# First feed-forward layer of chunk pairs by seven block products, with weight blocks kept in DRAM

## The chip, the cores and the metric

One core of a Trainium2 chip runs the whole kernel. The metric is the device time of one execution in microseconds (us); the time quoted for a kernel is the median of several executions. The engines are named as in the profile: PE is TensorE's matmul, PEld its weight load, DVE VectorE, ACT ScalarE, POOL GpSimd, SP SyncE, which here only issues DMAs.

## What is computed

```python
# attention: batch 4, heads 8, sequence 768, head dim 64, blocks of 64
for b in range(nb):                       # decayed linear attention
    intra = (qb @ kb.T * Dmask) @ vb
    inter = (qb * lam_pow) @ kv_state
    out[b] = intra + inter
    kv_state = lam_block * kv_state + (kb * rev_pow).T @ vb
# feed-forward on the 3072 tokens: d_model 512, d_ff 2048
x = attn_out.transpose(0, 2, 1, 3).reshape(3072, 512)
h = x @ w_in                              # 512 -> 2048, the first layer
g = softplus(h)
return g @ w_out                          # 2048 -> 512, the second layer
```

All is float32 in and out. Each of the large products is taken as three products of rounded parts: an operand is split in a high part (fp32r) and a low part (the rest, fp32r), and high·high, low·high and high·low are summed.

## The kernel before

The sequence is cut in `NCH` = 6 chunks of 128 positions; a chunk has 4 batches × 128 = 512 tokens. The hidden width is cut in `NF` = 16 blocks f of 128. A **step** s stands for chunk s // 16 and block s % 16, so there are 96 steps. The order is written by hand: every engine runs its instructions in the order in which the program emits them, and waits where a tile isn't there yet.

In step s the program emits, in this order: the decays of the attention unit that comes next, if one comes in step s + 1 (`k_decay` on ACT, `q_decay` on DVE); the softplus chain of step s − 1 (`chain_act` and `chain_hi` on ACT, `chain_lo` on DVE); up to step 16 the conversion of the weights (below); the second layer of step s − 4 (`mlp2`, 12 matmuls); an attention unit, if one is due; the first layer of step s (`mlp1`, 12 matmuls); and the DMA issues on SP's queue (`w_load`, `load_upto`).

**Attention** has 24 units g, one for each chunk and pair of heads (4 to a chunk). `mm_scores` and `mm_out` are runs of 64×64 matmuls. `mask_scores` and `update_states` follow `mm_scores` on DVE, and `mm_out` of a unit reads what both of them wrote. From unit 9 on, a unit is an event in `both_at`: in one step `mm_out` of unit g − 1 and `mm_scores` of unit g, every fourth step (g = 9 in step 19, g = 23 in step 75); `x_high` and `x_low` then write the high and low parts of the chunk's x. Unit 8 has its scores in step 17. `load_upto(n)` issues the loads of the units below n, two DMAs of 512 KB each; the load of unit 9 is emitted at the end of step 17.

**Weights** arrive as 64-bit words. Group j (two of the 32 weight blocks) is converted in step j and finished in step j + 1: `w_scale` and `w_round` on ACT, then `w_shift`, `w_sign`, `w_add` on DVE, and a step later `w_hi` on ACT and `w_lo` on DVE. In step s the emitted order is `w_hi` of group s − 1, `w_scale` and `w_round` of group s, `w_lo` of group s − 1, `w_shift`, `w_sign`, `w_add` of group s, and only then the attention unit's `mask_scores` and `update_states`. The last group, 15, is finished in step 16. The converted weights (16 tiles) stay in SBUF to the end.

**Buffers.** Tiles of 8 KB per partition come from one pool of 21 slots (`t8`): raw and converted weight pairs, x (two tiles to a chunk), attention units, output tiles. A tile's first writer waits until the last user of the slot's former tile is done. Tiles of 4 KB come from a pool of 7 (`t4`): the g of a step, conversion scratch. PSUM has four banks for the second layer's sums, two of kind `bank` (h, and an event's x and y), and one two-bank tile `work` (`mm_out`'s z, and the scores of the units outside events).

Of the kernel before, what the change touches and what calls it, by code (L numbers as in the profile page):

```python
# [31 lines left out]
def decay_attention_softplus_ffn(  # L32
# [264 lines left out]
    def mm_scores(g, x, y):  # L297
        q, k, kd, v = q_of(g), k_of(g), kds.pop(g), vt_of(g)
        if first_chunk(g):

            nc.tensor.matmul(y[lo], lhsT=warm[hi, :64], rhs=warm[hi], start=True, stop=False)
        for b in range(B):
            for t in range(2):
                cols = slice((2 * b + t) * 64, (2 * b + t + 1) * 64)
                for s in range(2):
                    r = half(s)
                    nc.tensor.matmul(x[r, cols], lhsT=k[r, b, t], rhs=q[r, b, t], start=True, stop=True)  # L307
                    if s == 0 or not last_chunk(g):
                        nc.tensor.matmul(  # L309
                            y[half(1 - s), cols], lhsT=kd[r, b, t], rhs=v[r, b, t],  # L310
                            start=s == 0 or not first_chunk(g), stop=s == 0 or not first_chunk(g),
                        )


    def mm_out(g, w):
        a, qd, v, st = aa.pop(g), qds.pop(g), vt_of(g), states[g]
        for b in range(B):
            cols = slice(b * 64, b * 64 + 64)
            for s in range(1 if first_chunk(g) else 0, 2):
                r = half(s)  # L320
                for t in range(2):
                    nc.tensor.matmul(w[half(t), s, cols], lhsT=st[r, b, t], rhs=qd[r, b, t], start=True, stop=False)  # L322
            for s in range(2):
                r = half(s)
                for t in range(2):
                    nc.tensor.matmul(  # L326
                        w[half(t), s, cols], lhsT=v[r, b, t], rhs=a[r, b, t],
                        start=s == 0 and first_chunk(g), stop=True,
                    )
# [45 lines left out]

    def x_low(g, w):
        x = x_of(g // NP, g % NP).rearrange("q n (b s i) -> q n s b i", b=B, s=2)
        nc.vector.tensor_sub(  # L378
            out=x[:, 1], in0=w[:, :, 0:256].rearrange("q s (b i) -> q s b i", b=B), in1=x[:, 0]
        )  # L380
# [4 lines left out]
    def chain_act(s):  # L385
        l_tiles[s] = tl([128, 512], F32, f"l{s}")
        nc.scalar.activation(l_tiles[s], h_tiles.pop(s), AF.Softplus)  # L387

    def chain_hi(s):
        g_tiles[s] = t4([128, 2, 512], F32R, f"g{s}")  # L390
        nc.scalar.copy(out=g_tiles[s][:, 0, :], in_=l_tiles[s])  # L391

    def chain_lo(s):
        g = g_tiles[s]
        nc.vector.tensor_sub(out=g[:, 1, :], in0=l_tiles.pop(s), in1=g[:, 0, :])  # L395

    def mlp1(s, ps_=range(NP)):
        c, f = divmod(s, NF)
        if s not in h_tiles:
            h_tiles[s] = bank(f"h{s}")  # L400
        w = w_of(f, 0)
        for p in ps_:
            cs = slice(p * 128, (p + 1) * 128)
            x = x_of(c, p)
            for n, (i, j) in enumerate(((0, 0), (1, 0), (0, 1))):
                nc.tensor.matmul(  # L406
                    h_tiles[s], lhsT=w[:, i, cs], rhs=x[:, j, :],
                    start=p == 0 and n == 0, stop=p == NP - 1 and n == 2,
                )

    def mlp2(ss):
        c = ss[0] // NF
        ends = ss[-1] % NF == NF - 1
        if ss[0] % NF == 0:
            o_tiles[c] = [obank(f"o{c}_{b}") for b in range(B)]
        if ends:
            ob = t8([128, B, 512], F32, f"ob{c}")
        for b in range(B):
            for s in ss:
                f = s % NF  # L420
                g, w = g_tiles[s], w_of(f, 1)
                for n, (i, j) in enumerate(((0, 0), (0, 1), (1, 0))):
                    nc.tensor.matmul(  # L423
                        o_tiles[c][b], lhsT=g[:, i, b * 128 : (b + 1) * 128], rhs=w[:, j],
                        start=f == 0 and n == 0, stop=f == NF - 1 and n == 2,
                    )
# [16 lines left out]
    xy, z = {}, {}  # L443
# [31 lines left out]

    last = NCH * NF
# [4 lines left out]
    outs_at[4 * NG - 17] = NG - 1  # L483
    units_at = {**scores_at, **both_at}
    for s in range(LAG, last + LAG):
        if s + 1 in units_at:
            k_decay(units_at[s + 1])
            q_decay(units_at[s + 1])
        if s - 1 < last:
            chain_act(s - 1)  # L490
            chain_hi(s - 1)
            chain_lo(s - 1)
# [12 lines left out]
        if s == last + LAG - 2:  # L505
            mlp2([s - LAG, s - LAG + 1])
        elif s - LAG < last - 1 and s - 1 not in both_at:
            mlp2([s - LAG])
        if s in scores_at:
            scores_of(scores_at[s])  # L510
            if scores_at[s] == 2 * NP:
                keep_values(2 * NP)
        if s in both_at:

            g = both_at[s]
            w, x, y = work(f"z{g - 1}"), bank(f"x{g}"), bank(f"y{g}")
            mm_out(g - 1, w)
            mm_scores(g, x, y)
            mask_scores(g, x)
            x_high(g - 1, w)  # L520
            update_states(g, y)
            x_low(g - 1, w)
            if g < NG - 1:
                keep_values(g)
# [52 lines left out]
```

## Time and profile before

| | us |
|---|---|
| median of 3 executions | 607.62 (607.26 to 607.64) |
| the profiled execution, first to last instruction | 606.2 |
| PE busy | 596.9 |
| DVE busy | 226.4 |
| ACT busy | 219.8 |
| POOL busy | 4.7 |

The profiled execution's span is 606.2 us; what lies around the instructions, some 1.4 us, is the difference to the median. A row of a group shows line, engine, operation, output<-input by the program's names, shape and count, then busy time in us and the mean of one in ns, then the engine's idle time ahead of these instructions and what ended it. A row of the timeline shows start in us, duration in us, engine, line, operation, and in brackets the idle time before it and what ended that. A busy PE is not PE at its peak, since matmuls overlap; so their pace is read from the distance between starts.

### The profile page before, as it was taken

Reading aid. Unit: us, or ns where it says so; the run is one execution under the profiler, and the core shown is the slowest. Engines: PE = TensorE matmul, PEld = TensorE weight load, DVE = VectorE, ACT = ScalarE, POOL = GpSimd, SP = SyncE. Lnnn points to the kernel's source line nnn. Section 1 sums busy time; section 2 is a strip of 40 time slices with the busy share of each in tenths; the row PEclk is TensorE's granted clock in tenths of the full one; section 3 lists DMA queues with packets and bytes.
Section 4 is the critical chain, followed back from the end, with each engine's and each line's share of the span. In section 5 each row is a group of like instructions: output and inputs, shape, how many; then the busy total and the mean of one; then the engine's idle time right before and its main releaser. Section 6 shows DMA issues by size and latency. Waiting matters only on the chain.

```text
span 606.2 us, 11776 instructions
## 1 busy us (share of the span) xinstructions
PE 596.9 (98%) x5299; PEld 488.5 (81%) x5299; DVE 226.4 (37%) x336; ACT 219.8 (36%) x355; POOL 4.7 (1%) x11
## 2 busy tenths in 40 slices
PE   9899999999999999999999999999999999999997
PEld 6577888888888888888888888888888888888886
DVE  7779999853232233132222321321312211211111
ACT  3777777633222223332223323222333121322121
POOL 3000000000000000000000000000000000000000
PEclk9999999999999999999999999999999999999999
DMA  8995314216002023300120500211500000100001
GB/s 297 406 406 227 122 74 141 88 52 208 3 2 70 1 70 98 112 2 11 61 70 29 182 2 0 71 32 40 207 3 1 1 1 1 69 2 0 1 0 69
DMA packets 15169, 48.98 MB, mean 81 GB/s; under 512 B 1808, under 2 KB 1808, under 8 KB 15120
## 3 DMA queue, kind: packets, MB, share of 16 engines
q1 hardware_dynamic: 14832, 47.72, 21.8%
q8 instruction: 41, 0.67, 0.4%
q10 hardware_dynamic: 288, 0.52, 0.2%
q14 instruction: 8, 0.07, 0.0%
HBM read 41.95 MB, written 6.29 MB: 80 GB/s over the span
## 4 chain that ended last, share of the span: by engine, by line
PE 91%; DMA 7%; DVE 1%; SPq 1%; ACT 0%; issue 0%
PE o L423 43%; PE h L406 41%; DMA raw<-in_wts 5%; PE z L322 2%; PE x L307 2%; DMA att<-in_att 2%; PE z L326 2%; PE w L307 1%; PE y L309 1%; SPq L84 0%; DVE w L238 0%; DVE c L231 0%; DVE c L225 0%; SPq L126 0%; ACT w L234 0%; PE w L309 0%
## 5 line engine op out<-in xcount | busy, mean ns | idle before, releaser
L423 PE MATMUL o<-w,g 128*128 128x512 f32 x1152 | 278.9, 391 | 1.1 <-DVE w L238 0.8
L406 PE MATMUL h<-x,w 128*128 128x512 f32 x1152 | 276.8, 391 | 0.0
L423 PEld LDWEIGHTS o<-w,g 128*128 128x128 f32 x1152 | 215.0, 188 | 47.2 <-DVE w L238 1.1
L406 PEld LDWEIGHTS h<-x,w 128*128 128x128 f32 x1152 | 215.1, 188 | 46.7 <-issue 1.2
L395 DVE TENSOR_TENSOR g<-l,g 128x512 fp32r<-128x512 f32 x96 | 66.4, 692 | 310.4 <-ACT g L391 310.2
L387 ACT ACTIVATE l<-h 128x512 f32<-128x512 f32 x96 | 57.4, 598 | 309.0 <-PE h L406 306.4
L391 ACT CAST g<-l 128x512 fp32r<-128x512 f32 x96 | 59.6, 621 | 3.1
L371 ACT CAST x<-z 128x512 fp32r<-128x512 f32 x24 | 14.0, 585 | 41.4 <-PE z L326 41.4
L334 DVE TENSOR_TENSOR a<-x,mask 128x512 f32<-128x512 f32 x15 | 10.4, 692 | 36.1 <-PE y L309 26.4
L339 DVE SCALAR_TENSOR_TENSOR st<-st,lam_c,y 64x256 f32<-64x256 f32 x52 | 22.9, 480 | 0.8
L322 PEld LDWEIGHTS z<-qd,st 64*64 64x64 f32 x640 | 17.0, 134 | 7.0 <-issue 7.0
L307 PE MATMUL x<-att 64*64 64x64 f32 x608 | 21.9, 219 | 0.0
L213 ACT ACTIVATE c<-raw 128x1024 f32<-128x1024 f32 (+1 forms) x19 | 19.0, 1001 | 7.3 <-DMA raw<-in_wts 7.3
L234 ACT CAST w<-c 128x1024 fp32r<-128x1024 f32 (+1 forms) x19 | 17.4, 914 | 10.3 <-DVE c L231 7.7
L238 DVE TENSOR_TENSOR w<-c,w 128x1024 fp32r<-128x1024 f32 (+1 forms) x19 | 20.0, 1053 | 2.8 <-ACT w L234 2.7
L231 DVE CUSTOM_DVE_ANT_0 c<-raw,c 128x2048 uint16<-128x2048 uint16 (+1 forms) x19 | 20.1, 1058 | 2.4
L322 PE MATMUL z<-qd,st 64*64 64x64 f32 x640 | 20.9, 224 | 0.0
L307 PEld LDWEIGHTS x<-att 64*64 64x64 f32 x608 | 20.0, 135 | 1.0 <-PE z L326 0.5
L225 DVE SCALAR_TENSOR_TENSOR c<-raw,c 128x1024 uint32<-128x1024 uint32 (+1 forms) x19 | 20.1, 1056 | 0.6
L378 DVE TENSOR_TENSOR x<-z,x 128x512 fp32r<-128x512 f32 x24 | 16.6, 690 | 7.9 <-ACT x L371 7.5
L217 ACT ACTIVATE raw<-raw 128x1024 uint32<-128x1024 uint32 (+1 forms) x19 | 18.9, 993 | 0.0
L285 ACT ACTIVATE kd<-att,rp 128x256 f32<-128x256 f32 x40 | 18.1, 502 | 0.0
(54 smaller groups left out, 230.5 us busy)
## 6 DMA issues: line engine op xcount, KB each, us to landing
att<-in_att SPq DMA_DIRECT2D x48, 512.0 KB, 5.5
raw<-in_wts SPq DMA_DIRECT2D x32, 512.0 KB, 10.2
out_dram<-ob SPq DMA_DIRECT2D x22, 256.0 KB, 2.2
out_dram<-ob ACTq DMA_DIRECT2D x2, 256.0 KB, 2.0
lam_b<-in_lam SPq DMA_DIRECT2D x1, 4.0 KB, 2.6
```

Source lines behind the costliest of these rows:

```text
L213: nc.scalar.activation(c.bitcast(F32), raw_at(ks, 1).bitcast(F32), AF.Copy, scale=2.0**-112)
L225: nc.vector.scalar_tensor_tensor(out=c, in0=raw_at(ks, 1), scalar=0x80000000, in1=c, op0=ALU.bitwise_and, op1=ALU.bitwise_or)
L231: nc.vector.tensor_add(out=c, in0=c, in1=raw_at(ks, 0))
L238: nc.vector.tensor_sub(out=w[:, 1], in0=conv.pop(ks[0]).bitcast(F32), in1=w[:, 0])
L307: nc.tensor.matmul(x[r, cols], lhsT=k[r, b, t], rhs=q[r, b, t], start=True, stop=True)
L322: nc.tensor.matmul(w[half(t), s, cols], lhsT=st[r, b, t], rhs=qd[r, b, t], start=True, stop=False)
L339: nc.vector.scalar_tensor_tensor(out=to[:, :, t], in0=of[:, :, t], scalar=lam_c[r, h : h + 1], in1=u[:, :, t], op0=ALU.mult, op1=ALU.add,)
L387: nc.scalar.activation(l_tiles[s], h_tiles.pop(s), AF.Softplus)
L391: nc.scalar.copy(out=g_tiles[s][:, 0, :], in_=l_tiles[s])
L395: nc.vector.tensor_sub(out=g[:, 1, :], in0=l_tiles.pop(s), in1=g[:, 0, :])
L406: nc.tensor.matmul(h_tiles[s], lhsT=w[:, i, cs], rhs=x[:, j, :], start=p == 0 and n == 0, stop=p == NP - 1 and n == 2,)
L423: nc.tensor.matmul(o_tiles[c][b], lhsT=g[:, i, b * 128 : (b + 1) * 128], rhs=w[:, j], start=f == 0 and n == 0, stop=f == NF - 1 and n == 2,)
```

## The change

The step loop ends after two chunks (`STD` = 2), 32 steps. Chunks 2+3 and 4+5 go in pairs: for 8 pairs of hidden blocks, the 2×2 block product (two hidden blocks by two chunks, the contraction of 512 cut in two halves) is formed by seven products of sums of blocks, `P1` to `P7`, in place of eight. A product is 6 matmuls (2 slices of the contraction × 3 parts). Their sums of outputs run on PSUM and DVE. The second layer of the first chunk of a pair is emitted among the products of the next iteration (`rest`); that of the second chunk follows in a loop of its own, whose softplus outputs wait in SBUF.

The blocks of w_in and their sums S1 to S4, split in parts, and w_out, go to DRAM tiles `g1`, `g2`, `g3` during steps 8 to 31 (`store_blocks`, `block_sums` on POOL, `store_sums`), and are loaded again in each iteration (`load_w1`, `load_w2`). In SBUF only the iteration's blocks are held.

The attention events come twice as often: unit 8's scores in step 15 in place of 17, units 9 to 16 every second step from 16 to 30, and units 17 to 23 one to an iteration of the first pair. The load of unit 9 is emitted at the end of step 14. For chunks 2 to 5 `x_raw` copies x unsplit, and `x_sums_early`, `x_sums_late` and `x_block` form and split the sums of x (T1 to T4) on DVE and ACT.

```diff
+STD = 2
+    dr = ctx.enter_context(tc.tile_pool(name="dr", bufs=1, space=bass.MemoryType.DRAM))
...
+    g1 = [dr.tile([128, 2, 4, 256], F32, name=f"g1_{i}", tag=f"g1_{i}") for i in range(NF // 2)]
+    g2 = [dr.tile([128, 2, 3, 256], F32, name=f"g2_{i}", tag=f"g2_{i}") for i in range(NF // 2)]
+    g3 = [dr.tile([128, 2, 2, DM], F32, name=f"g3_{i}", tag=f"g3_{i}") for i in range(NF // 2)]
...
+    def block_sums(i):
+        full = t4([128, 2, DM], F32, f"full{i}")
+        for n in range(2):
+            w = w_of(2 * i + n, 0)
+            nc.gpsimd.tensor_add(out=full[:, n], in0=w[:, 0], in1=w[:, 1])
...
+        sums = block_parts[i] = t4([128, 4, 256], F32, f"sums{i}")
+        nc.gpsimd.tensor_add(out=s1, in0=a21, in1=a22)
+        nc.gpsimd.tensor_sub(out=s3, in0=a11, in1=a21)
+        nc.gpsimd.tensor_sub(out=s2, in0=s1, in1=a11)
+        nc.gpsimd.tensor_sub(out=s4, in0=a12, in1=s2)
+    def store_sums(i):
+        sums = block_parts.pop(i)
+        parts = t8([128, 2, 4, 256], F32R, f"parts{i}")
+        nc.scalar.copy(out=parts[:, 0], in_=sums)
+        nc.vector.tensor_sub(out=parts[:, 1], in0=sums, in1=parts[:, 0])
...
+    def load_w1(i):
+        a, b = t8([128, 2, 4, 256], F32R, f"w1a{i}"), t8([128, 2, 3, 256], F32R, f"w1b{i}")
+        nc.sync.dma_start(out=a.bitcast(F32), in_=g1[i])
+        nc.sync.dma_start(out=b.bitcast(F32), in_=g2[i])
...
+    def product(name, i, to, start=True):
+        a, n = W_AT[name]
+        w, x = w1_tiles[i][a], xc[name]
+        for p in range(2):
+            for m, (k, j) in enumerate(((0, 0), (1, 0), (0, 1))):
+                nc.tensor.matmul(
+                    to, lhsT=w[:, k, n, p * 128 : (p + 1) * 128], rhs=x[:, j, p],
+                    start=start and p == 0 and m == 0, stop=p == 1 and m == 2, skip_group_check=True,
+                )
...
-    scores_at[NF + 1] = 2 * NP
-    both_at = {4 * g - 17: g for g in range(2 * NP + 1, NG)}
+    scores_at[NF - 1] = 2 * NP
+    both_at = {2 * g - 2: g for g in range(2 * NP + 1, 4 * NP + 1)}
...
         if s in units_at:
             load_upto(units_at[s] + 2)
+        if s == NF - 2:
+            load_upto(2 * NP + 2)
+        if 8 <= s < 8 + NF:
+            store_blocks(s - 8)
+        if s >= NF and s % 2 == 0:
+            block_sums((s - NF) // 2)
+        if s >= NF and s % 2:
+            store_sums((s - NF) // 2)
...
+        for i in range(NF // 2):
+            if i + 1 < NF // 2:
+                load_w1(i + 1)
+            load_w2(i)
+            unit = nxt if more else None
+            if unit is not None and unit < NG:
+                k_decay(unit)
+                q_decay(unit)
...
+            product("P1", i, a)
+            nc.scalar.copy(out=p1, in_=a)
+            product("P6", i, b_)
+            nc.vector.tensor_add(out=u2, in0=b_, in1=p1)
+            product("P5", i, c_)
+            product("P2", i, a, False)
+            la = tl([128, 512], F32, f"la{c}_{i}")
+            nc.scalar.activation(la, a, AF.Softplus)
+            ga = parts_of(f"g{c}_{2 * i}", la)
+            product("P7", i, b_, False)
+            nc.vector.tensor_add(out=u3, in0=b_, in1=p1)
+            nc.vector.tensor_add(out=u3, in0=c_, in1=u3)
+            nc.scalar.activation(lb[2 * i + 1], u3, AF.Softplus)
+            low_of(ga, la)
+            run(rest, 2)
+            product("P4", i, b_, False)
+            nc.vector.tensor_add(out=c21, in0=b_, in1=p1)
+            nc.scalar.activation(c21, c21, AF.Softplus)
+            gb = parts_of(f"g{c}_{2 * i + 1}", c21)
+            product("P3", i, c_, False)
+            nc.vector.tensor_add(out=u2, in0=c_, in1=u2)
+            nc.scalar.activation(lb[2 * i], u2, AF.Softplus)
+            run(rest, 4)
+            if unit is not None and unit <= NG:
+                event(unit)
+                load_upto(unit + 2)
+                nxt += 1
+            low_of(gb, c21)
+            run(rest)
+            pair = [(2 * i + n, (ga, gb)[n], w2_tiles[i][:, n]) for n in range(2)]
+            rest = seconds(c, pair, i == NF // 2 - 1)
```

More of the change, by code (lines that the diff above doesn't have):

```diff
@@ L374, in x_high, with x_raw @@
         )
+    xr = {}
+    def x_raw(g, w):
+        c, p = divmod(g, NP)
+        if c not in xr:
+            xr[c] = t8([128, NP, 512], F32, f"xr{c}")
+        nc.scalar.copy(
+            out=xr[c][:, p].rearrange("q (b s i) -> q s b i", b=B, s=2),
+            in_=w[:, :, 0:256].rearrange("q s (b i) -> q s b i", b=B),
+        )
     def x_low(g, w):
@@ new lines, in decay_attention_softplus_ffn, with x_sums_early, x_sums_late @@
+    t_sums = {}
+    def x_sums_early(c, n):
+        out = t_sums[n] = t8([128, 4, 512], F32, f"tt{c}_{n}")
+        nc.vector.tensor_sub(out=out[:, 0], in0=xr[c + 1][:, n], in1=xr[c][:, n])
+        x_block("P5", out[:, 0], n)
+    def x_sums_late(c, n):
+        tt = t_sums.pop(n)
+        b12, b22, b21 = xr[c + 1][:, n], xr[c + 1][:, 2 + n], xr[c][:, 2 + n]
+        nc.vector.tensor_sub(out=tt[:, 1], in0=b22, in1=tt[:, 0])
+        nc.vector.tensor_sub(out=tt[:, 2], in0=b22, in1=b12)
+        nc.vector.tensor_sub(out=tt[:, 3], in0=b21, in1=tt[:, 1])
+        x_block("P6", tt[:, 1], n)
+        x_block("P7", tt[:, 2], n)
+        x_block("P4", tt[:, 3], n)
+        x_block("P3", b22, n)
@@ new lines, in product, with parts_of @@
+    def product(name, i, to, start=True):
[6 more added lines that the diff above has]
+                    start=start and p == 0 and m == 0, stop=p == 1 and m == 2, skip_group_check=True,
+                )
+    def parts_of(name, l):
+        g = t4([128, 2, 512], F32R, name)
+        nc.scalar.copy(out=g[:, 0], in_=l)
+        return g
@@ new lines, in low_of, with second, finish @@
+    def low_of(g, l):
+        nc.vector.tensor_sub(out=g[:, 1], in0=l, in1=g[:, 0])
+    outs, obs = {}, {}
+    def second(c, f, b, g, w):
+        if (c, b) not in outs:
+            outs[c, b] = obank(f"o{c}_{b}")
+        for n, (i, j) in enumerate(((0, 0), (0, 1), (1, 0))):
+            nc.tensor.matmul(
+                outs[c, b], lhsT=g[:, i, b * 128 : (b + 1) * 128], rhs=w[:, j],
+                start=f == 0 and n == 0, stop=f == NF - 1 and n == 2,
+            )
+    def finish(c, b):
+        if c not in obs:
+            obs[c] = t8([128, B, 512], F32, f"ob{c}")
+        copy = nc.vector.tensor_copy if b % 2 else nc.scalar.copy
+        copy(out=obs[c][:, b], in_=outs[c, b])
+        queue = nc.scalar if c == NCH - 1 and b % 2 == 0 else nc.sync
+        queue.dma_start(out=out[b * S + c * C : b * S + (c + 1) * C, :], in_=obs[c][:, b])
@@ new lines, in seconds, with run @@
+    def seconds(c, fs, ends=False):
+        work_ = []
+        for f, g, w in fs if not ends else ():
+            work_ += [lambda f=f, g=g, w=w, b=b: second(c, f, b, g, w) for b in range(B)]
+        if ends:
+            for b in range(B):
+                for f, g, w in fs:
+                    work_.append(lambda f=f, g=g, w=w, b=b: second(c, f, b, g, w))
+                work_.append(lambda b=b: finish(c, b))
+        return work_
+    def run(work_, n=None):
+        for _ in range(len(work_) if n is None else min(n, len(work_))):
+            work_.pop(0)()
@@ L479, in decay_attention_softplus_ffn, with event @@
+    last = STD * NF
     scores_at = {3 * n + 3: NP + n for n in range(NP)}
     outs_at = {s + 2: g for s, g in scores_at.items()}
-    scores_at[NF + 1] = 2 * NP
-    both_at = {4 * g - 17: g for g in range(2 * NP + 1, NG)}
-    outs_at[4 * NG - 17] = NG - 1
+    scores_at[NF - 1] = 2 * NP
+    both_at = {2 * g - 2: g for g in range(2 * NP + 1, 4 * NP + 1)}
     units_at = {**scores_at, **both_at}
-    for s in range(LAG, last + LAG):
+    def event(g):
+        w = work(f"z{g - 1}")
+        mm_out(g - 1, w)
+        if g < NG:
+            x, y = bank(f"x{g}"), bank(f"y{g}")
+            mm_scores(g, x, y)
+            mask_scores(g, x)
+        x_raw(g - 1, w)
+        if g < NG:
+            update_states(g, y)
+            keep_values(g)
@@ L486, in decay_attention_softplus_ffn @@
+    for s in range(LAG, last):
         if s + 1 in units_at:
@@ L488, in decay_attention_softplus_ffn @@
             q_decay(units_at[s + 1])
[L489 to L492, printed above, removed]
+        chain_act(s - 1)
+        chain_hi(s - 1)
+        chain_lo(s - 1)
         old, new = w_group(s - 1), w_group(s)
@@ L504, in decay_attention_softplus_ffn @@
             w_add(*new)
-        if s == last + LAG - 2:
-            mlp2([s - LAG, s - LAG + 1])
-        elif s - LAG < last - 1 and s - 1 not in both_at:
+        if s - 1 not in both_at:
             mlp2([s - LAG])
@@ L513, in decay_attention_softplus_ffn @@
         if s in both_at:
[L515 to L524, printed above, removed]
+            event(both_at[s])
             mlp2([s + 1 - LAG])
@@ L536, in decay_attention_softplus_ffn @@
             load_upto(units_at[s] + 2)
+        if s == NF - 2:
[6 more added lines that the diff above has]
+            store_sums((s - NF) // 2)
+        for at, name, n in ((23, "P1", 0), (23, "P1", 1), (25, "P2", 0), (25, "P2", 1)):
+            if s == at:
+                x_block(name, xr[2][:, n + (2 if name == "P2" else 0)], n)
+        if s == last - 3:
+            x_sums_early(2, 0)
@@ new lines, in decay_attention_softplus_ffn, with old_seconds @@
+        if s == last - 2:
+            x_sums_late(2, 0)
+            load_w1(0)
+        if s == last - 1:
+            x_sums_early(2, 1)
+    x_sums_late(2, 1)
+    chain_act(last - 1)
+    chain_hi(last - 1)
+    chain_lo(last - 1)
+    def old_seconds(ss, ends=False):
+        return seconds(STD - 1, [(s % NF, g_tiles[s], w_of(s % NF, 1)) for s in ss], ends)
+    for b in range(B):
+        outs[STD - 1, b] = o_tiles[STD - 1][b]
+    run(old_seconds([last - 4, last - 3]))
+    rest = old_seconds([last - 2, last - 1], True)
@@ new lines, in decay_attention_softplus_ffn, with split @@
+    nxt = 4 * NP + 1
+    for c in range(STD, NCH, 2):
+        more = c + 2 < NCH
+        lb = {}
+        gs = {}
+        for i in range(NF // 2):
[6 more added lines that the diff above has]
+                q_decay(unit)
+            if i % 2 == 0:
+                l4 = t8([128, 4, 512], F32, f"lb{c}_{i}")
+            for n in range(2):
+                lb[2 * i + n] = l4[:, 2 * (i % 2) + n]
+            ta, tb = t4([128, 2, 512], F32, f"ta{c}_{i}"), t4([128, 2, 512], F32, f"tb{c}_{i}")
+            p1, u2, u3, c21 = ta[:, 0], ta[:, 1], tb[:, 0], tb[:, 1]
+            a, bc = bank(f"a{c}_{i}"), work(f"bc{c}_{i}")
+            b_, c_ = bc[:, 0], bc[:, 1]
+            product("P1", i, a)
[29 more added lines that the diff above has]
+            rest = seconds(c, pair, i == NF // 2 - 1)
+        ahead = 2
+        def split(f):
+            gs[f] = parts_of(f"g{c + 1}_{f}", lb[f])
+            low_of(gs[f], lb[f])
+        for f in range(ahead):
+            split(f)
+        for i in range(2):
+            load_w2(i)
+        run(rest)
+        xc.clear()
+        steps = []
+        if more:
+            steps = [lambda n=n, m=m: x_block(n, xr[c + 2][:, m + (2 if n == "P2" else 0)], m) for n in ("P1", "P2") for m in range(2)]
+            for n in range(2):
+                steps += [lambda n=n: x_sums_early(c + 2, n), lambda n=n: x_sums_late(c + 2, n)]
+        for f in range(NF - 2):
+            if f % 2 == 0 and f // 2 + 2 < NF // 2:
+                load_w2(f // 2 + 2)
+            if f + ahead < NF:
+                split(f + ahead)
+            if f >= 1:
+                run(steps, 1)
+            if f == 9 and more:
+                load_w1(0)
+            run(seconds(c + 1, [(f, gs.pop(f), w2_tiles[f // 2][:, f % 2])]))
+        rest = seconds(c + 1, [(f, gs[f], w2_tiles[f // 2][:, f % 2]) for f in (NF - 2, NF - 1)], True)
@@ L539, in _layout @@
+    run(rest)
 def _layout(q, k, v, lam, w_in, w_out):
```

31 lines of the change are left out of this document (28 added, 3 removed).

## The prediction

> **What bounds the kernel now.** I read the page's busy line first, then the chain that ended last, then the costliest groups, and at last the timeline of single engines where the change moves work.
>
> ```profile
> PE 596.9 (98%) x5299; PEld 488.5 (81%) x5299; DVE 226.4 (37%) x336; ACT 219.8 (36%) x355; POOL 4.7 (1%) x11
> PE 91%; DMA 7%; DVE 1%; SPq 1%; ACT 0%; issue 0%
> L423 PE MATMUL o<-w,g 128*128 128x512 f32 x1152 | 278.9, 391 | 1.1 <-DVE w L238 0.8
> L406 PE MATMUL h<-x,w 128*128 128x512 f32 x1152 | 276.8, 391 | 0.0
> ```
>
> PE is busy for 98% of the span and makes 91% of the chain; its two large groups idle 1.1 us in all. So a matmul that goes shortens the span by its pace, as long as nothing new makes PE wait. The pace isn't the 391 ns of the rows, as matmuls overlap. It is read from the chain in order of time, whose columns are start, length and what ran:
>
> ```profile
> 144.71 5.44 PE h L406 x24
> ...
> 168.82 5.44 PE h L406 x24
> ...
> 591.58 10.89 PE o L423 x48
> ```
>
> 48 matmuls take 10.89 us and 24 take 5.44: **0.2267 us each**, for both layers, although the second layer changes its PSUM bank every three matmuls. From one event to the next, four steps on, it is 168.82 - 144.71 = 24.11 us; four steps of 24 matmuls are 21.76, so an event costs PE 2.35 us. The change keeps the number of events, so their cost stays.
>
> **What is removed.** The first layer of chunks 2 to 5 has 4 x 16 x 12 = 768 matmuls now. After it is 2 pairs x 8 iterations x 7 products x 6 = 672. So 96 matmuls go: 96 x 0.2267 = **21.8 us**. The second layer keeps its 1152. Whether PE gives all of this to the span depends on what it may have to wait for, place by place.
>
> **Inside an iteration** (the handing over of PSUM). The sums on DVE and ACT cost what the rows of the same size show:
>
> ```profile
> L395 DVE TENSOR_TENSOR g<-l,g 128x512 fp32r<-128x512 f32 x96 | 66.4, 692 | 310.4 <-ACT g L391 310.2
> L387 ACT ACTIVATE l<-h 128x512 f32<-128x512 f32 x96 | 57.4, 598 | 309.0 <-PE h L406 306.4
> L391 ACT CAST g<-l 128x512 fp32r<-128x512 f32 x96 | 59.6, 621 | 3.1
> L339 DVE SCALAR_TENSOR_TENSOR st<-st,lam_c,y 64x256 f32<-64x256 f32 x52 | 22.9, 480 | 0.8
> L285 ACT ACTIVATE kd<-att,rp 128x256 f32<-128x256 f32 x40 | 18.1, 502 | 0.0
> ```
>
> An iteration is 42 + 24 = 66 matmuls, 14.96 us, and with an event 17.3. DVE has seven operations of 0.69 in it (u2 twice, u3 twice, c21, two low parts), 4.8 us, and with an event 3.3 more (mask 0.69, four updates of 0.48, q_decay 0.69): 8.1 of 17.3. ACT has 4 evictions or softplus at 0.6 and so on, seven operations, 4.3 us, and 2.2 with an event. Neither is a bound. The tightest handing over is P4, which accumulates on P7's bank and must wait until DVE has read it into u3: six second-layer matmuls lie between, 1.36 us, against one DVE operation of 0.69 and two wake-ups. A wake-up from PE to ACT is near 0.04 us in the trace (the h group that starts at 121.87 and lasts 2.88 ends at 124.75, ACT starts at 124.79; both rows stand further down). I take nothing; the bound is 0.5 us in each of 16 iterations, 8 us, if a wake-up were half a microsecond.
>
> **The reloads.** Per iteration SP loads 1.05 + 0.79 MB of w_in blocks and sums and 1.05 MB of w_out, in the first pair also a unit of 1.05 MB: 3.93 MB in 17.3 us, 227 GB/s; in the second pair 2.88 MB in 14.96 us, 193 GB/s; in the loops of the second chunk 1.05 MB per 5.44 us, 193 GB/s.
>
> ```profile
> GB/s 297 406 406 227 122 74 141 88 52 208 3 2 70 1 70 98 112 2 11 61 70 29 182 2 0 71 32 40 207 3 1 1 1 1 69 2 0 1 0 69
> DMA to landing us min/median/max: 3.4/4.9/7.8
> ```
>
> The first row is the page's, 40 slices; the second is of the issues of attention loads from 140 to 480 us. The second and third slices held 406 GB/s of loads, so the need is about half of what the queue has shown, and each load is issued an iteration ahead. Stores (22 MB over steps 8 to 31, some 149 us, 148 GB/s) have less need. Cost: nothing.
>
> **The entry to the first pair.** After the last x of unit 15, DVE and ACT form 7 sums and parts for each half of T1 to T4. Counting from the end of the scores in step 30, DVE has mask and updates (2.6), `x_sums_late` (4.8), the step's low part, the split of the last block sums (1.2), `x_sums_early` (1.4) and two operations more of the second `x_sums_late` ahead of P6's: some 14 us. PE has 12 + 12 + 12 + 24 + 6 + 3 matmuls ahead of the one that needs it, 15.6 us. It fits by about 1.5 us, so I take nothing, with a bound of 4 us, the whole of an `x_sums_late` late.
>
> **Steps 14 to 16.** Here the change moves work onto work, and here I expect a wait. Unit 8's scores and the event of unit 9 come in steps 15 and 16 (17 and 19 before), while weight groups 14 and 15 are still being converted. Rows of ACT, DVE, PE and SP's queue from the timeline of the kernel before, and one of the waits of SP's queue:
>
> ```profile
> 110.99 1.05 ACT L234 CAST w<-c 128x1024 fp32r<-128x1024 f32 x1 [2.59 <-PE z L326]
> 116.56 1.06 ACT L234 CAST w<-c 128x1024 fp32r<-128x1024 f32 x1 [0.81 <-DVE c L231]
> 119.59 0.91 ACT L285 ACTIVATE kd<-att,rp 128x256 f32<-128x256 f32 x2
> 124.79 0.60 ACT L387 ACTIVATE l<-h 128x512 f32<-128x512 f32 x1 [1.60 <-PE h L406]
> 115.30 1.23 DVE L231 CUSTOM_DVE_ANT_0 c<-raw,c 128x2048 uint16<-128x2048 uint16 x1
> 116.44 0.68 DVE L378 TENSOR_TENSOR x<-z,x 128x512 fp32r<-128x512 f32 x1
> 117.65 1.23 DVE L238 TENSOR_TENSOR w<-c,w 128x1024 fp32r<-128x1024 f32 x1
> 118.79 0.69 DVE L221 TENSOR_SCALAR c<-c 128x1024 uint32<-128x1024 uint32 x1
> 119.52 1.22 DVE L225 SCALAR_TENSOR_TENSOR c<-raw,c 128x1024 uint32<-128x1024 uint32 x1
> 120.88 1.23 DVE L231 CUSTOM_DVE_ANT_0 c<-raw,c 128x2048 uint16<-128x2048 uint16 x1
> 129.34 1.79 DVE L339 SCALAR_TENSOR_TENSOR st<-st,lam_c,w 64x256 f32<-64x256 f32 x4
> 113.71 2.88 PE L423 MATMUL o<-w,g 128*128 128x512 f32 x12
> 116.43 2.88 PE L406 MATMUL h<-x,w 128*128 128x512 f32 x12
> 121.87 2.88 PE L406 MATMUL h<-x,w 128*128 128x512 f32 x12
> 124.59 2.88 PE L423 MATMUL o<-w,g 128*128 128x512 f32 x12
> 128.50 3.02 PE L406 MATMUL h<-x,w 128*128 128x512 f32 x12
> 119.35 0.80 SPq L84 DMA_DIRECT2D att<-in_att  x2
> SPq L84 <- PE h L406: 9.3, 1, 9.3
> ```
>
> The 21 slots of 8 KB are all taken in step 14: weight pairs 0 to 13, four x tiles, unit 8, the raw words of groups 14 and 15. The rows confirm it: `w_hi` of group 13 waited 2.59 us for `mm_out` of unit 7 (110.99), and the load of unit 9 waited 9.3 us, to 119.35, for the end of step 15's first layer (116.43 + 2.88), which frees chunk 0's x. After the change that load is emitted in step 14. It is the first to ask for the slot of raw group 14, free when `w_add` 14 ends, 115.30 + 1.23 = 116.5. In the kernel before, `w_hi` 14 started at that very moment (116.56), on that slot; now it must wait for chunk 0's x.
>
> Now the chain, in the times of this trace. Issue of the load 116.55, of its second half about 116.95, landing 4.9 later: 121.85. In ACT's order `k_decay` 9 stands ahead of the softplus chain of step 14, and that ahead of `w_hi` 14: 0.91 + 0.62 + 0.62, so `w_hi` 14 starts near 124.0 (its slot is free by 121.2). From `w_hi` 14 to the end of `w_add` 15 it is 120.88 + 1.23 - 116.56 = 5.55 us, at the same spacing. Queued behind that on DVE are `mask_scores` 8 (0.69) and the first two updates of the state (2 x 0.45), which `mm_out` 8 reads: 124.0 + 7.15 = **131.2**.
>
> PE meanwhile: second layer of step 11 at 113.71, to 116.43; the scores of unit 8 need the `work` tile, which `x_low` 7 frees at 117.12 (0.7 late); they take 128.50 - (124.59 + 2.72) = 1.2; first layer of step 15 with 2.85, to 121.2; second layer of step 12, to 123.9. Then `mm_out` 8 must wait until 131.2: **7.3 us**, and 0.7 before. With landings of 3.4 and 7.8 us in place of 4.9 the stall is 5.8 or 10.2. Afterwards DVE and ACT catch up: an event comes every 13.2 us, in which DVE has some 7 us. The loads of units 10 to 12 come a step ahead of their use behind the stores of `parts`; I find them 4 to 8 us ahead of what PE needs.
>
> POOL's sums are 2 + 4 operations every two steps:
>
> ```profile
> 6.80 1.84 POOL L292 TENSOR_TENSOR own<-att,lp 64x512 f32<-64x512 f32 x1 [4.40 <-DVE lam_c L183]
> 10.59 1.28 POOL L292 TENSOR_TENSOR own<-att,lp 64x512 f32<-64x512 f32 x1 [1.95 <-DMA att<-in_att]
> ```
>
> At 1.56 us for 512 columns and half for 256 that is 6.2 us of 13.2; it stays hidden.
>
> The Trainium skill, "SBUF — State Buffer", section "Who interferes with whom", says that a DVE instruction with two SBUF inputs and a GpSimd instruction that reads SBUF exclude each other, the later one blocking fully. The first four-part sum of POOL would fall on the stretch of `w_lo`, `w_sign`, `w_add`; by the rule, three waits of up to 0.8 us (half of 1.56) would make the stall up to 2.4 us longer, 596.3. The trace of before has POOL at work in its first 12 us alone and doesn't decide it.
>
> **The sum.** 607.6 - 21.8 + 0.7 + 7.3 = **593.8, say 594 us**. The profiled execution spans 606.2, its median stands 1.4 higher, and the new span would be 592.4.
>
> **Rivals.**
>
> 1. *No stall in step 16*, if unit 9's load finds another slot or group 15's conversion is ordered earlier than I count: 607.6 - 21.8 = 586 to 588. Against it stands the full table of slots. Chance 0.16.
>
> 2. *The stall slows PE behind it.* The longest wait of PE in the list of waits is 1.4 us (the row gives the sum, the count and the longest), so no long one is shown; but its first matmuls have a slow start:
>
> ```profile
> PE z L326 <- issue: 2.4, 2, 1.4
> 1.45 7.12 PE L146 MATMUL warm_ps<-warm 128*128 128x512 f32 x18 [1.45 <-DVE warm L141]
> ```
>
> 18 matmuls took 7.12 us where the later pace gives 4.08. If 7 us of waiting bring that back, up to 3.0 us are added: 595 to 597. Chance 0.26. This is the rule of the Trainium skill, "TensorE: Matmul & The Clock Gate", section "What's actually happening": after an idle window of about 3.4 us the clock halves, and a window of work restores it; by its figures, as an estimate, 1.7 us.
>
> 3. *The handing over of PSUM isn't covered*: 0.3 to 0.8 us in each of 16 iterations, 5 to 13 us beside the stall: 599 to 607. For it speaks the short cover of P4, against it the small wake-up. Chance 0.08.
>
> 4. *Slower than before: the reloads come late.* All of it hangs on the rate of loads while stores and output run beside them. The gain that is left, 13.7 us, is used up where the rate falls to about 207 GB/s (3.93 MB then takes 19.0 in place of 17.3 us, eight times). At 180 GB/s an iteration of the first pair takes 21.8 and one of the second 16.0 us: +36 and +8, 638 us. The 406 GB/s speak against it; that no store of this size is in the trace leaves it open. Chance 0.06.
>
> The forecast has 0.42; 0.02 is left for something else. The range leaves out rival 4 and the upper half of rival 3, and reaches to rival 1: **586 to 601**, about 0.86 by these cases, which I leave so, since the stall's size is unsure on both sides. Faster by over 0.2% (what can be told from no change) has 0.91, within it 0.02, slower 0.07.
>
> **What would show it.** Right: 96 fewer matmuls of the first layer; steps and products at 0.2267 us; one PE idle of 6 to 10 us near 124 us, ahead of z, ended by DVE, with `k_decay` 9 waiting for the load of unit 9; the granted clock after it tells rival 2. Wrong: PE waiting ahead of P4 or P7 on DVE (rival 3), or weight loads of the products waiting on DMA (rival 4), or POOL ending most waits of ACT's copy in `store_sums`.

## The result and the profile after

| | us | ratio to before, 95% interval |
|---|---|---|
| before | 607.63 (607.26 to 607.76) | |
| changed | **651.35** (649.75 to 651.98) | 1.0716 [1.07, 1.0731] |

Each row is the median of four executions, with the lowest and the highest.

The change makes the kernel 7% slower; 594 was forecast, with 586 to 601 as the range. The profiled execution took 651.41 us, its span is 649.6.

From the page of the changed kernel, the busy line and the chain by engine:

```profile
PE 595.5 (92%) x5203; PEld 469.9 (72%) x5203; DVE 307.4 (47%) x452; ACT 251.6 (39%) x408; POOL 51.2 (8%) x59
PE 63%; DVE 13%; DMA 13%; ACT 4%; SPq 3%; issue 3%; DVEq 0%; ACTq 0%
```

The matmuls are fewer, as meant (5299 to 5203), yet PE has 92% of the span where it had 98%, and 63% of the chain where it had 91%. DVE, which made 1% of the chain, makes 13%. The list of PE's waits (sum, count, longest) says where:

```profile
PE bc L577 <- DVE ta L737: 15.4, 16, 2.6
PE bc L577 <- DVE tb L750: 12.5, 16, 0.8
PE o L436 <- ACT w L236: 6.2, 2, 5.8
PE y L311 <- ACT l L400: 5.0, 4, 1.8
```

Two waits come 16 times, once in each iteration of the pairs. L737 is DVE's u2, which reads P6's sum in `b_`; L750 is c21, which reads P4's sum in `b_`. One iteration of the second pair, PE's timeline and then DVE's two rows:

```profile
473.09 1.52 PE L577 MATMUL a<-xcP,w1a 128*128 128x512 f32 x6
474.45 1.52 PE L577 MATMUL bc<-xcP,w1a 128*128 128x512 f32 x6
476.83 1.65 PE L577 MATMUL bc<-xcP,w1a 128*128 128x512 f32 x6 [0.85 <-DVE ta L737]
478.32 1.52 PE L577 MATMUL a<-xcP,w1a 128*128 128x512 f32 x6
479.68 1.52 PE L577 MATMUL bc<-xcP,w1b 128*128 128x512 f32 x6
481.04 1.52 PE L596 MATMUL o<-w,g 128*128 128x512 f32 x6
482.71 1.67 PE L577 MATMUL bc<-xcP,w1b 128*128 128x512 f32 x6 [0.15 <-DVE tb L745]
485.17 1.66 PE L577 MATMUL bc<-xcP,w1b 128*128 128x512 f32 x6 [0.78 <-DVE tb L750]
486.66 4.25 PE L596 MATMUL o<-w,g 128*128 128x512 f32 x18
490.75 1.52 PE L577 MATMUL a<-xcP,w1a 128*128 128x512 f32 x6
...
476.08 0.69 DVE L737 TENSOR_TENSOR ta<-bc,ta 128x512 f32<-128x512 f32 x1 [2.10 <-PE bc L577]
484.42 0.69 DVE L750 TENSOR_TENSOR tb<-bc,ta 128x512 f32<-128x512 f32 x1 [1.17 <-PE bc L577]
```

The third row is P5. It writes `c_`, the other bank of `bc`, and needs nothing that u2 makes; yet it starts at 476.83, just behind u2 (476.08 + 0.69 = 476.77). The distance from P6 is 2.38 us where six matmuls take 1.36. P3 (485.17) stands in the same way behind c21. Summed from start to start, P5 comes 1.02 late, P4 0.31, P3 1.10, and the groups behind P5 and P3 0.13 each: 2.7 us. The iteration takes 490.75 - 473.09 = 17.66 where 66 matmuls need 14.96. The rows' bracketed idle time (0.85, 0.78) shows only part of that; the distance between starts counts it all.

The second place is steps 16 to 30, PE's timeline:

```profile
117.99 3.02 PE L419 MATMUL h<-x,w 128*128 128x512 f32 x12
126.81 0.80 PE L436 MATMUL o<-w,g 128*128 128x512 f32 x1 [5.81 <-ACT w L236]
128.08 5.06 PE L436 MATMUL o<-w,g 128*128 128x512 f32 x11 [0.47 <-DVE w L240]
136.57 3.04 PE L436 MATMUL o<-w,g 128*128 128x512 f32 x12
139.45 5.60 PE L419 MATMUL h<-x,w 128*128 128x512 f32 x24
...
239.19 5.60 PE L419 MATMUL h<-x,w 128*128 128x512 f32 x24
```

The first row is the first layer of step 15; it ends in effect at 117.99 + 2.85 = 120.84. A second layer (2.72) and an event (2.35) on, at 125.9, the next second layer should start; it starts at 136.57: 10.7 us. From 139.45 to 239.19 seven rounds of two steps and an event should take 7 x 13.23 = 92.6; they take 99.7: 7.1 us.

The account: the profile before without the 96 matmuls would span 606.2 - 21.8 = 584.4; 649.6 is 65.2 more. Of these 16 x 2.7 = 43.2 are the waits inside the iterations, 10.7 is step 16, 7.1 the later events, and 3.5 the second iteration, which took 23.4 us (269.97 to 293.37 between the starts of P1) against 19.9 of the others with an event. That leaves 0.7, and PE's wait ahead of the scores of unit 8 is 0.64.

### The profile page after: what moved, and what is told of

It is laid out like the page before. It is cut to its first block, busy times and chain, and to the rows that moved or that the text cites. A ratio compares the mean times of both kernels' runs of the same rounds, so it can differ in the third digit from the quotient of the medians.

```text
span 649.6 us, 11970 instructions
## 1 busy us (share of the span) xinstructions
PE 595.5 (92%) x5203; PEld 469.9 (72%) x5203; DVE 307.4 (47%) x452; ACT 251.6 (39%) x408; POOL 51.2 (8%) x59
## 3 DMA queue, kind: packets, MB, share of 16 engines
HBM read 104.86 MB, written 29.36 MB: 207 GB/s over the span
## 4 chain that ended last, share of the span: by engine, by line
PE 63%; DVE 13%; DMA 13%; ACT 4%; SPq 3%; issue 3%; DVEq 0%; ACTq 0%
PE o L596 24%; PE bc L577 19%; DMA att<-in_att 9%; PE a L577 6%; PE o L436 5%; PE h L419 5%; DMA raw<-in_wts 3%; DVE tb L744 2%; DVE tb L745 2%; DVE tb L750 2%; DVE ta L737 2%; PE z L324 1%; DVE parts L526 1%; ACT parts L525 1%; SPq L86 1%
## 5 line engine op out<-in xcount | busy, mean ns | idle before, releaser
L419 PE MATMUL h<-x,w 128*128 128x512 f32 x384 | 93.4, 394 | 0.0
L577 PE MATMUL bc<-xcP,w1b 128*128 128x512 f32 x288 | 77.5, 404 | 14.9 <-DVE tb L750 12.5
L419 PEld LDWEIGHTS h<-x,w 128*128 128x128 f32 x384 | 71.0, 188 | 16.7 <-issue 1.2
L577 PEld LDWEIGHTS bc<-xcP,w1b 128*128 128x128 f32 x288 | 51.7, 188 | 38.3 <-DVE tb L750 19.4
L577 PE MATMUL bc<-xcP,w1a 128*128 128x512 f32 x192 | 51.3, 403 | 15.4 <-DVE ta L737 15.4
L577 PEld LDWEIGHTS bc<-xcP,w1a 128*128 128x128 f32 x192 | 34.9, 188 | 28.8 <-DVE ta L737 22.2
L577 PE MATMUL a<-xcP,w1a 128*128 128x512 f32 x192 | 50.0, 397 | 0.0
L744 DVE TENSOR_TENSOR tb<-bc,ta 128x512 f32<-128x512 f32 x16 | 11.1, 692 | 73.1 <-PE bc L577 73.1
L577 PEld LDWEIGHTS a<-xcP,w1a 128*128 128x128 f32 x192 | 36.9, 192 | 8.0
L737 DVE TENSOR_TENSOR ta<-bc,ta 128x512 f32<-128x512 f32 x16 | 11.1, 692 | 60.0 <-PE bc L577 58.0
L408 DVE TENSOR_TENSOR g<-l,g 128x512 fp32r<-128x512 f32 x32 | 23.2, 724 | 25.0 <-ACT g L404 24.8
L512 POOL TENSOR_TENSOR full<-w 128x512 f32<-128x512 f32 x16 | 21.4, 1360 | 117.9 <-PE o L436 114.7
```

The costliest lines, as they stand in the source:

```text
L419: nc.tensor.matmul(h_tiles[s], lhsT=w[:, i, cs], rhs=x[:, j, :], start=p == 0 and n == 0, stop=p == NP - 1 and n == 2,)
L512: nc.gpsimd.tensor_add(out=full[:, n], in0=w[:, 0], in1=w[:, 1])
L577: nc.tensor.matmul(to, lhsT=w[:, k, n, p * 128 : (p + 1) * 128], rhs=x[:, j, p], start=start and p == 0 and m == 0, stop=p == 1 and m == 2 ...
L737: nc.vector.tensor_add(out=u2, in0=b_, in1=p1)
L744: nc.vector.tensor_add(out=u3, in0=b_, in1=p1)
```

## The experiments

**Theory A** for the 43 us: `b_` and `c_` are the two banks of one tile, and the program's waits are set by tile; so a product on one bank waits for a read of the other. **Rival B**: a bank that DVE reads is handed back late in itself. **Rival C**: the reloads are late. For step 16, **theory D**: the early load of unit 9 takes the slot that weight group 14 needs, and holds ACT's queue.

### e1_reorder: the order of emission alone

```diff
             product("P6", i, b_)
-            nc.vector.tensor_add(out=u2, in0=b_, in1=p1)
             product("P5", i, c_)
+            nc.vector.tensor_add(out=u2, in0=b_, in1=p1)
...
             product("P4", i, b_, False)
+            product("P3", i, c_, False)
             nc.vector.tensor_add(out=c21, in0=b_, in1=p1)
             nc.scalar.activation(c21, c21, AF.Softplus)
             gb = parts_of(f"g{c}_{2 * i + 1}", c21)
-            product("P3", i, c_, False)
```

> Only the emission order in an iteration of the pairs changes: P5 stands ahead of DVE's read of P6's sum, and P3 ahead of DVE's read of P4's sum; same tiles, same instructions. Theory A (the two banks of bc are one tile, so a product on one bank waits for DVE's read of the other): in the changed kernel's iteration of 17.66 us P5 comes 1.02 late, P3 1.10, and the groups right behind them 0.13 each; these 2.38 go, 16 times, 38 us: 613 us, iteration 15.3. P4's 0.3 stays, as two reads of the tile still stand ahead of it. Rival B (the handing over itself: a bank that DVE has read comes back late, whatever stands beside it): the waits move to P7 and the next P6, and the time stays at 645 to 652. Rival C (the late reloads and the attention loads of the pairs make the loss): no change, 651.

Measured 615.79 us, ratio 1.0134 [1.0108, 1.016]: 35.6 us gone. The PE timeline of an iteration:

```profile
436.14 1.52 PE L577 MATMUL a<-xcP,w1a 128*128 128x512 f32 x6
437.50 2.88 PE L577 MATMUL bc<-xcP,w1a 128*128 128x512 f32 x12
...
444.61 3.02 PE L577 MATMUL bc<-xcP,w1b 128*128 128x512 f32 x12 [0.15 <-DVE tb L745]
...
451.55 1.52 PE L577 MATMUL a<-xcP,w1a 128*128 128x512 f32 x6
```

P6 and P5 now run as twelve without a gap, and so do P4 and P3. The iteration takes 451.55 - 436.14 = 15.41, and the one wait that is left is P4's, for the read of `c_` in L745, as theory A has it. The waits did not move to P7 or the next P6: rival B falls. Nothing of the loads has changed: rival C falls for these 36 us.

### e2_two_tiles: one tile for each bank, the order unchanged

```diff
-        return ps.tile([128, 2, 512], F32, tag="t", bufs=1, name=name)
+        return [ps.tile([128, 512], F32, tag=f"t{n}", bufs=1, name=f"{name}_{n}") for n in range(2)]
...
-            b_, c_ = bc[:, 0], bc[:, 1]
+            b_, c_ = bc
...
-        nc.scalar.copy(
-            out=xr[c][:, p].rearrange("q (b s i) -> q s b i", b=B, s=2),
-            in_=w[:, :, 0:256].rearrange("q s (b i) -> q s b i", b=B),
-        )
+        for n in range(2):
+            nc.scalar.copy(
+                out=xr[c][:, p].rearrange("q (b s i) -> q s b i", b=B, s=2)[:, n],
+                in_=w[n][:, 0:256].rearrange("q (b i) -> q b i", b=B),
+            )
```

> The emission order of the changed kernel stays; the two-bank tile of the scores, z and the products is two tiles of one bank each (the copies of z out of PSUM become two of half the size). Theory A: P5 and P3 no longer wait for a read of the other bank, nor P4 for the second sum: 2.7 us less in each of 16 iterations, 43 us, 608 us, up to 3 more where the smaller copies hinder ACT. Rival B: P5 and P3 wait as before, 651. Rival C: 651.

Measured 605.16 us, ratio 0.996 [0.9945, 0.9976]: 46.2 us gone, with every product in its old place.

PE's timeline of an iteration, and then DVE's row of u2:

```profile
430.45 1.52 PE L580 MATMUL a<-xcP,w1a 128*128 128x512 f32 x6
431.81 2.88 PE L580 MATMUL bc<-xcP,w1a 128*128 128x512 f32 x12
...
438.62 2.88 PE L580 MATMUL bc<-xcP,w1b 128*128 128x512 f32 x12
...
445.42 1.52 PE L580 MATMUL a<-xcP,w1a 128*128 128x512 f32 x6
...
433.44 0.69 DVE L740 TENSOR_TENSOR ta<-bc,ta 128x512 f32<-128x512 f32 x1 [14.99 <-PE bc L580]
```

The iteration is 14.97 us, the 66 matmuls and nothing else. DVE reads `b_` (433.44) while PE writes `c_` in the second half of the twelve from 431.81, at full pace; so it was never the chip that kept the banks apart, but the unit by which the program waits. P4's wait is gone too, since the read of `c_` no longer counts against `b_`. Of the 3 us beyond theory A's 43, 2.6 are the second iteration's: it takes 18.1 us here, 0.9 more than the first, where in the changed kernel it took 3.5 more than the others.

### e3_late_events and e6_decay_own_step: steps 14 to 30

```diff
 # e3_late_events; e6_decay_own_step has the part from "if s + 1 in units_at" on alone
-    scores_at[NF - 1] = 2 * NP
-    both_at = {2 * g - 2: g for g in range(2 * NP + 1, 4 * NP + 1)}
+    scores_at[NF] = 2 * NP
+    both_at = {min(2 * g, last - 1): g for g in range(2 * NP + 1, 4 * NP + 1)}
...
             event(both_at[s])
+            load_upto(both_at[s] + 2)
...
-        if s == NF - 2:
-            load_upto(2 * NP + 2)
...
-        if s + 1 in units_at:
-            k_decay(units_at[s + 1])
-            q_decay(units_at[s + 1])
+        if s + 1 in scores_at:
+            k_decay(scores_at[s + 1])
+            q_decay(scores_at[s + 1])
         chain_act(s - 1)
         chain_hi(s - 1)
         chain_lo(s - 1)
+        if s in both_at:
+            k_decay(both_at[s])
+            q_decay(both_at[s])
```

In e3_late_events the event of unit 16 falls in step 31 and takes the second layer of step 28 along, so that one is left out behind the step loop.

> The iterations stay as in the changed kernel. Unit 8's scores come in step 16 in place of 15, units 9 to 15 in steps 18 to 30, unit 16 in step 31; a unit's decays are emitted in its own step behind the softplus chain, and the next unit's load right behind the event. Theory D (the load of unit 9 takes the slot of raw group 14, so that the weight conversion, and with it the second layer of step 12, waits): the PE idle of 10.5 us in step 16 goes, and most of the 7.3 us that events lose up to step 30, in which ACT stands at the decay for a late load: 634 to 638. Rival (the stretch is slow because stores crowd the queue and POOL blocks DVE, whatever the order): 645 to 651.

e3_late_events measured 636.25 us, ratio 1.0471 [1.045, 1.0492]: 15.1 us gone, and the waits inside the iterations stay (15.4 us on u2 and 12.5 us on c21 in its list of waits). So the two causes are separate.

> From the changed kernel, with one edit: an event's decays are emitted in the event's own step, behind the softplus chain, in place of the step before; the loads and the steps of the events stay. Theory D1 (ACT's queue: the conversion of group 14 stands behind a decay that waits for unit 9's load): ACT is no longer held in step 15, the conversion of group 14 starts when chunk 0's x frees its slot, some 3 to 5 us earlier; the stall of step 16 shrinks from 10.5 to about 5, and the events up to step 30 lose little: 636 to 641. Theory D2 (the slot is what binds, and the queue makes no difference): the stall of step 16 stays near 10 and only the later events gain: 644 to 647.

e6_decay_own_step measured 640.21 us, ratio 1.0534 [1.0513, 1.0555]: 11.1 us gone by the place of the decays alone. ACT's row of `k_decay` 9 in the changed kernel, and then, in e6_decay_own_step, ACT's row of `w_hi` 14 and PE's wait in step 16:

```profile
123.78 0.91 ACT L287 ACTIVATE kd<-att,rp 128x256 f32<-128x256 f32 x2 [9.52 <-DMA att<-in_att]
```

```profile
120.05 1.05 ACT L236 CAST w<-c 128x1024 fp32r<-128x1024 f32 x1 [4.27 <-PE h L419]
...
PE z L324 <- DVE st L341: 3.7, 1, 3.7
```

In the changed kernel ACT stood 9.5 us for unit 9's load, and everything behind it in its queue stood too, the conversion of group 14 among it. With the decays behind, `w_hi` 14 waits for the first layer of step 15 (PE h): that is the slot. PE stalls 3.7 us ahead of `mm_out` 8 and 0.76 us inside the second layer of step 12. Counted as above, the second layer behind the event is due at 126.3 and starts at 130.9: step 16 loses 4.6 us in place of 10.7. So ACT's queue made the larger part of the stall, and the slot with DVE's queue behind it the rest; no run tells these two apart. The seven rounds behind take 92.5 us (133.79 to 226.27), so the later events lose nothing. The run gains less than these 6.1 and 7.1 us together, as the second iteration's wait grew from 2.6 to 3.8 us and the clock was at one half once more (last section). In e3_late_events, with the later steps, the longest wait in step 16 is 1.9 us.

### e4_both, e5_pool_later, e7_decay_in_pair: the rest

e4_both puts e1_reorder and e3_late_events together, with three second-layer groups ahead of P4 in place of two.

> The order of e1_reorder and the schedule of e3_late_events together, and three second-layer groups ahead of P4 in place of two. If the two causes are separate and P4's wait goes too: 651 - 38 - 5 - 15 = 593, some 14 us under the kernel before. If one hides the other: 600 to 612.

Measured **592.33 us**, ratio 0.9743 [0.9726, 0.9759]. The iteration is 14.96 us, with no wait in the second pair. A wait of 1.93 us is left in step 16. Rows of PE, DVE and POOL there, and then PE's granted clock, the column behind the count in brackets, in windows of 1 us:

```profile
121.08 4.24 PE L436 MATMUL o<-w,g 128*128 128x512 f32 x11 [1.93 <-DVE w L240]
116.65 1.53 DVE L294 TENSOR_TENSOR qd<-att,lp 128x512 f32<-128x512 f32 x1
118.10 1.78 DVE L408 TENSOR_TENSOR g<-l,g 128x512 fp32r<-128x512 f32 x1
116.33 3.00 POOL L512 TENSOR_TENSOR full<-w 128x512 f32<-128x512 f32 x2 [104.39 <-PE o L436]
...
122.00:123.00 1.00, 1.00 (x5) 0.53 0.81 217
...
124.00:125.00 1.00, 1.00 (x4) 0.50 0.99 383
...
126.00:127.00 1.00, 1.00 (x38) 1.00 1.03 376
```

While POOL sums (116.33 to 119.33), two DVE operations take 1.53 and 1.78 in place of 0.69 us, and PE waits for what is behind them. PE then runs at half its clock for over 3 us. What that costs can be read from e3_late_events, which has the same wait at the same place, while its clock stays at 1.00:

```profile
121.07 2.79 PE L436 MATMUL o<-w,g 128*128 128x512 f32 x11 [1.93 <-DVE w L240]
```

The 11 matmuls take 2.79 in place of 4.24 us, and the first layer behind them starts at 124.88 in place of 126.43: 1.55 us.

```diff
-        if s >= NF and s % 2 == 0:
-            block_sums((s - NF) // 2)
-        if s >= NF and s % 2:
-            store_sums((s - NF) // 2)
+        if s > NF and s % 2 == 0:
+            store_sums((s - NF) // 2 - 1)
+        if s >= NF and s % 2:
+            block_sums((s - NF) // 2)
...
+    store_sums(NF // 2 - 1)
```

> From e4_both, with POOL's sums of the blocks and their stores emitted one step later. In e4_both the second layer of step 12 still waits 1.93 us for the low part of group 14, while q_decay takes 1.53 and the chain's low part 1.78 us in place of 0.69, both beside POOL's first two sums. Theory E (POOL's reads of SBUF hold up DVE's operations with two SBUF inputs): these go back to 0.69 in that stretch, the wait goes, and with it the lower clock behind it: 588 to 590. Rival (DVE is only late by the order of its own queue): 592, the wait stays.

Measured 591.16 us, ratio 0.9723 [0.9706, 0.9739], where 588 to 590 was expected. The executions (590.39 to 592.05) overlap those of e4_both (591.35 to 593.74), so the gain isn't settled by the times. The mechanism is settled by the rows of e5_pool_later, DVE's and then POOL's:

```profile
116.78 0.68 DVE L294 TENSOR_TENSOR qd<-att,lp 128x512 f32<-128x512 f32 x1
117.38 0.69 DVE L408 TENSOR_TENSOR g<-l,g 128x512 fp32r<-128x512 f32 x1
119.84 2.20 DVE L227 SCALAR_TENSOR_TENSOR c<-raw,c 128x1024 uint32<-128x1024 uint32 x1
...
119.37 3.80 POOL L512 TENSOR_TENSOR full<-w 128x512 f32<-128x512 f32 x2 [107.30 <-DVE w L240]
```

POOL's sums start 3 us later; the two operations that they had slowed are back at 0.68 and 0.69, and `w_sign`, which they now meet, takes 2.20 in place of 1.22. PE's wait of 1.93 us in step 16 is gone, and the clock stays at 1.00 there, so the rival falls. (The 0.8 us for DVE w that its list of waits still has come before 100 us and stand in the kernel before as well.) But at 223.79 PE now waits 1.53 us for a `k_decay` where it waited 0.56 in e4_both, and behind that the clock is at one half from 225 to 227 us; so part of what was won is lost again there.

e7_decay_in_pair moves `k_decay` and `q_decay` of an iteration behind `low_of(ga, la)`.

> From e5_pool_later, with the decays of units 17 to 23 moved from the start of an iteration to behind the low part of the first hidden block. In e4_both ACT's copy of P1's sum came 1.44 us late in the second iteration, behind a decay that waited for its load. If that is the whole of it: 1.5 to 2.5 us less than e5_pool_later. If the load is late for the scores too: no change.

Measured **590.28 us**, ratio 0.9711 [0.9692, 0.973], the fastest run of the study and some 17 us under the kernel before. Against e5_pool_later it is 0.9 us, again within the spread of the executions; its span is 0.9 us shorter (589.4 against 590.3), as long as the wait of P2 for P1's copy (0.9 us) that stands in e5_pool_later's list of waits and not in that of e7_decay_in_pair.

I expected 1.5 to 2.5; the wait had been 1.44 in e4_both and was 0.9 in e5_pool_later, so less was left to win. Its page's first line shows PE back at its old share:

```profile
PE 577.6 (98%) x5203; PEld 471.4 (80%) x5203; DVE 310.3 (53%) x452; ACT 251.1 (43%) x408; POOL 51.9 (9%) x59
```

## Why the prediction was wrong, step by step

- **The matmuls removed: right.** The count falls by 96 and the pace is the one forecast: 14.96 us for the 66 matmuls of an iteration in e4_both, 14.97 in e2_two_tiles. Of the 21.8 us, e7_decay_in_pair keeps 17.5 (607.75 - 590.28).
- **Inside an iteration: wrong, and this is the step that failed.** It took nothing, with a bound of 8 us, and named P4 the tightest place. It looked for hazards by bank: who writes the bank that DVE reads? P5 and P3 write another bank, so they didn't appear. But the program waits by tile, and `b_` and `c_` are one tile. P5 had no matmul at all between P6 and itself to cover the read, P3 none behind P4. P4's own wait, for which the step had looked, is 0.31 us. Rival 3 named the kind of wait but priced it at 0.3 to 0.8 us per iteration; it is 2.7, and 43 of the 65 us.
- **The reloads: right for the weights, wrong for one attention load.** Rival 4, the one on the slower side, did not happen: no product waited for a weight load in the list of PE's waits. But not every load is issued an iteration ahead. The load of unit 18 is issued at 266.56, at the end of the first iteration, and its decay stands at the start of the second, which begins at 269.97:

```profile
273.32 0.91 ACT L287 ACTIVATE kd<-att,rp 128x256 f32<-128x256 f32 x2 [3.92 <-DMA att<-in_att]
```

  ACT's copy of P1's sum comes behind it, so u2 is late and P5 waits 2.62 us: with the clock (below) this is the second iteration's 3.5 us. Two figures of the prediction are a little off and change nothing: the stores are 23.1 MB (the profile's page has 29.36 MB written, against 6.29 before), not 22, and the chances of the cases inside the range add to 0.88, not 0.86.
- **Steps 14 to 16: the mechanism right, the size small.** The table of slots held: ACT stood 9.5 us at `k_decay` 9 for unit 9's load, and PE's wait ahead of the scores is 0.64 where 0.7 was forecast. PE stopped a stage earlier than I had it, as the second layer of step 12 itself waits for group 14. What ended the stall is the forecast chain to `mm_out` 8, here in rows of the changed kernel:

```profile
125.72 1.04 ACT L236 CAST w<-c 128x1024 fp32r<-128x1024 f32 x1
...
130.44 1.54 DVE L233 CUSTOM_DVE_ANT_0 c<-raw,c 128x2048 uint16<-128x2048 uint16 x1
...
132.61 1.79 DVE L341 SCALAR_TENSOR_TENSOR st<-st,lam_c,w 64x256 f32<-64x256 f32 x4
...
134.55 0.34 PE L324 MATMUL z<-qd,st 64*64 64x64 f32 x8 [1.41 <-DVE st L341]
```

  `mm_out` 8 is due at 120.84 + 2.72 = 123.6 and starts at 134.55, 11.0 us late; 7.3 was forecast. `w_hi` 14 starts 4.9 us behind the first layer of step 15 (2.8 forecast), since the load landed later. From there to the end of `w_add` 15 it is 6.3 us (5.55 forecast), with `w_sign` at 1.64 and `w_add` at 1.54 us beside POOL's sums. And `mm_out` 8 starts behind all four updates of the state, 2.6 us on, not behind two (1.6 forecast).
- **The later events: wrong by 7.1 us.** I had their loads 4 to 8 us ahead of what PE needs. But the decays stood a step ahead of the scores in ACT's queue, and the issues from 110 to 260 us took longer to land than those I had used (median 6.3 us against 4.9), beside the stores; so ACT waited at the decays:

```profile
  ACT kd L287: 57.3, 7
...
DMA to landing us min/median/max: 4.1/6.3/7.2
```

  ACT's late softplus then held the h bank, on which the next unit's scores wait (PE y <- ACT l, 5.0 us in the list of PE's waits). The place of the decays is what decides: in e6_decay_own_step the loads land no sooner (median 7.0), and these events lose nothing.
- **The entry to the first pair: right.** The first iteration shows only the waits of the others.
- **POOL stays hidden: right for the sums, wrong for DVE.** It did not end a wait of PE itself, but it slowed DVE's operations. In e4_both two of them take 1.53 and 1.78 us in place of 0.69 beside POOL's sums, and in e5_pool_later the slowing moves along with the sums. The rule of the Trainium skill, "SBUF — State Buffer", section "Who interferes with whom", has it that a DVE operation with two SBUF inputs and a POOL operation that reads SBUF shut each other out. The traces agree in that both are slowed; that one holds the other up for its whole length isn't shown.
- **Rival 2, the slower clock behind a stall: it came, but in step 16 it cost nothing.** Windows of 1 us in the changed kernel, with the granted clock as the column behind the count:

```profile
126.00:127.00 1.00, 0.18 (x1) 0.65 0.09 34
...
132.00:133.00 1.00, 1.00 (x3) 0.50 0.91 127
...
134.00:135.00 1.00, 0.45 (x29) 1.00 1.03 404
```

  Half the clock for over 6 us: the 11 matmuls at 128.08 take 5.06 us. But behind them PE still waits 1.41 us for DVE's updates (the row at 134.55), so faster matmuls would only have waited longer. The clock did cost time in the second iteration: from the start of P5 to that of P7 PE takes 4.44 us (275.48 to 279.92), where the first iteration takes 2.85. That is 1.6 of its 3.5 us; the forecast left the clock to the rival, at up to 3.0.

## What to carry to other kernels

Before a chain of sums is put on two halves of one buffer, ask by what unit the program tracks who may write: where it is the tile, a write to one half waits for the reads of the other, and either two tiles or an order with both writes ahead of both reads takes the wait away (46 and 36 us here). A matmul group of 1.36 us covers one DVE read only if it stands between that read's start and the next write; count the cover for each write, not for each bank. When work is moved into a stretch that still fills its buffers, look up which transfer now asks for a slot first, and which instructions stand behind the one that waits for it.

## What the runs showed of the hardware that I had not expected

The granted clock fell to one half after short idle times: in e4_both after 1.93 us (0.50 to 0.53 for some 3 us), in the changed kernel's second iteration after 2.62 us (0.50 from 277 to 279 us), and after 5.81 us in step 16. The waits of 0.8 us, two in each iteration, left it at 1.00 in the second pair. The Trainium skill, "TensorE: Matmul & The Clock Gate", section "What's actually happening", gives one idle window of about 3.4 us as what halves the clock; here less was enough.

Nor does the length of one wait decide it. e3_late_events has the same wait of 1.93 us in step 16 as e4_both, and e6_decay_own_step has one of 3.68 us there, and behind both the clock stayed at 1.00. In e6_decay_own_step it fell at 31 us behind a wait of 1.43 us, which e4_both has too (1.45) without a fall. What else decides it stays open.
